# Bank-by-bank first and last chunks, a smaller first load of V and rearranged final stores in a grouped-query attention kernel

## The chip, the cores and the metric

The kernel runs on one core of a Trainium2 chip. The metric is device time of one execution in microseconds (us). Before the change three runs gave a median of 522.89 us (522.8 to 523.7). A run's time stands about 1.75 us above the span of its trace (524.22 against 522.5, 523.1 against 521.4), so the two can be turned into each other. The rounds of the experiments ran on four chips (numbers 8, 3, 15 and 5 in the record), so a time is compared with that of the kernel before in the same rounds; medians over all rounds mix chips.

## The reference

```python
B, Hq, Hkv, Sq, Sk, D = 16, 32, 8, 288, 512, 128      # bf16
k = jnp.repeat(k, Hq // Hkv, axis=1)
v = jnp.repeat(v, Hq // Hkv, axis=1)
scores = jnp.einsum("bhqd,bhkd->bhqk", q, k) * D ** -0.5
p = softmax(scores, axis=-1)
return jnp.einsum("bhqk,bhkd->bhqd", p, v)
```

## The kernel before

There are 128 groups (a batch and a head of K and V). The four heads of Q of a group are 9 tiles of 128 rows. The scores are computed transposed, keys on the partitions, in 3 chunks of 1536 columns (three PSUM banks) a group, 384 chunks in all. TensorE computes chunk n's scores, ScalarE exponentiates them into SBUF, and TensorE multiplies a batch of 3 tiles by V three chunks later. V carries a column of ones, so the sum of a row comes with the product; VectorE takes its reciprocal and evicts. For 62 of the chunks VectorE also computes 120 columns of the exponential. Parts that the argument touches, with cuts marked:

```python
# the first transfers of the sync engine (q0: Q of group 0 in two parts)
first = [lambda i=i: op_q0(i) for i in range(2)]
first += [lambda: op_q(1), lambda: op_k(0, 2), lambda: op_q(2), lambda: op_v(0, None, 2, UG), lambda: op_q(3)]
# and of ScalarE's queue
op_kd(eng, 0); ...; op_kd(eng, 1)            # K of groups 0 and 1, transposed by TensorE
op_v(0, eng, 0, 2)                           # V of groups 0 and 1

# TensorE
for n in range(NS):
    if n == 2: op_warm(4, P, ps_o[:, 0])
    op_s(n)                                  # scores: wait for K, Q and the exponential of chunk n-2
    ...
    if n == 2: op_kt(1, range(NJ), 1)        # transposes of K of group 1; VectorE copies them
    if n >= LAG: op_pv(n - LAG)              # batch n-3 times V
...
# sync engine, at the very end
eng.wait_ge(sem["s_flag"], 1)
eng.load(reg, flag_i[:])
for (s, n) in need(eng, stored()):           # 12 waits: every buffer of the output, and the last stores
    eng.wait_ge(s, n)
eng.br_ne(reg, 0, ...)                       # a rare other path if a sum was out of range
```

## Time and profile before

| | before, first profile |
|---|---|
| time of the profiled execution, span | 524.22, 522.5 us |
| median of three timed runs | 522.89 us |
| TensorE, ScalarE busy | 510.6, 513.4 us |
| Q of group 1 lands | 9.74 us |
| first P times V matmul | 10.52 us |
| last eviction ends | 520.00 us |
| from there to the end of the span | 2.48 us |

The kernel has three parts: a start until TensorE and ScalarE are both full, a steady state, and a tail after the last eviction. The first P times V matmul and the end of the last eviction mark the borders. The lines of the page and of the views stand in the prediction.

### The profile page before, as it was taken

To read this page: it belongs to the slowest core of one execution; us is meant where nothing else is said; L and a number is where in the kernel's file an instruction comes from. 1 tells how busy PE (TensorE), PEld (TensorE's weight loads), DVE (VectorE), ACT (ScalarE), POOL (GpSimd) and SP (SyncE) were. 2 spreads that over 40 slices of the span, in tenths; PEclk is the share of its full clock that TensorE was granted. 3 is DMA by queue.
4 is the path that set the end of the run, shared out by engine and by line. 5 is a ranking of instruction groups with operands and counts; after the bars stand their busy time and mean duration, and the time that the engine had idled before them with its cause. 6 is when DMAs were issued, how large, how long until landed. Compare 5 with 4: busy or idle time off the path is not lost.

```text
span 522.5 us, 15279 instructions
## 1 busy us (share of the span) xinstructions
PE 510.6 (98%) x6124; PEld 395.5 (76%) x6230; DVE 363.0 (69%) x1309; ACT 513.4 (98%) x389; POOL 79.8 (15%) x135
## 2 busy tenths in 40 slices
PE   7999999999999999999999999999999999999997
PEld 4777777777777777777777777777777777777776
DVE  1767677677677677676776776767767767767765
ACT  6999999999999999999999999999999999999996
POOL 2111111111111111111111111111111111111110
PEclk9999999999999999999999999999999999999999
DMA  8999999899899999998999999999999999997212
GB/s 174 246 219 242 260 188 226 208 225 260 208 202 273 224 184 266 241 204 219 205 267 214 199 226 230 232 230 203 238 195 235 224 218 210 205 211 179 77 69 92
DMA packets 253109, 110.05 MB, mean 211 GB/s; under 512 B 219760, under 2 KB 236784, under 8 KB 253040
## 3 DMA queue, kind: packets, MB, share of 16 engines
q1 hardware_dynamic: 252480, 108.56, 96.7%
q8 instruction: 49, 0.80, 0.7%
q10 hardware_dynamic: 560, 0.52, 0.5%
q14 instruction: 20, 0.16, 0.1%
HBM read 17.04 MB, written 37.75 MB: 105 GB/s over the span
## 4 chain that ended last, share of the span: by engine, by line
PE 96%; DMA 1%; issue 1%; SPq 0%; DVE 0%
PE ps_o L446 50%; PE ps_s L409 45%; DMA qt_sb<-in_q_dram 1%; PE ps_o L420 1%; SPq L316 0%; DVE o_sb L550 0%; DVE rl_sb L540 0%; DVE o_sb L560 0%; PE ps_o L636 0%; DVE bad_sb L586 0%; DVE flag_i L705 0%; DVE bad_sb L583 0%
## 5 line engine op out<-in xcount | busy, mean ns | idle before, releaser
L481 ACT ACTIVATE pt_sb<-ps_s 128x1536 bf16<-128x1536 f32 (+2 forms) x385 | 510.9, 1444 | 1.4 <-PE ps_s L409 1.4
L446 PE MATMUL ps_o<-v_sb,pt_sb 128*128 128x129 bf16 x4596 | 322.9, 220 | 1.3 <-DVE o_sb L550 0.2
L446 PEld LDWEIGHTS ps_o<-v_sb,pt_sb 128*128 128x128 bf16 x4596 | 283.7, 98 | 49.9 <-DVE o_sb L550 0.4
L409 PE MATMUL ps_s<-qt_sb,kt_sb 128*128 128x512 bf16 (+2 forms) x1430 | 290.6, 320 | 6.4 <-DMA qt_sb<-in_q_dram 1.9
L550 DVE TENSOR_TENSOR o_sb<-ps_o,rl_sb 128x384 bf16<-128x384 f32 x383 | 212.6, 555 | 8.9
L409 PEld LDWEIGHTS ps_s<-qt_sb,kt_sb 128*128 128x128 bf16 x1536 | 124.0, 98 | 63.5 <-ACT pt_sb L481 2.2
L540 DVE RECIPROCAL rl_sb<-ps_o 128x3 f32<-128x3 f32 x383 | 68.5, 179 | 137.0 <-PE ps_o L446 137.0
L533 POOL COPY v_sb<-vd_sb 128x512 bf16<-128x512 bf16 x128 | 78.8, 616 | 430.5 <-PE ps_o L446 416.2
L514 DVE SCALAR_TENSOR_TENSOR u_sb<-u_sb,m_sb 128x120 f32<-128x120 f32 x124 | 34.5, 278 | 0.0
L521 DVE SCALAR_TENSOR_TENSOR pt_sb<-u_sb,e_sb 128x120 bf16<-128x120 f32 x62 | 17.5, 283 | 2.1
L514 DVE SCALAR_TENSOR_TENSOR u_sb<-m_sb 128x120 f32<-128x120 f32 x62 | 17.2, 277 | 0.0
L492 DVE TENSOR_SCALAR y_sb<-ps_o 128x120 f32<-128x120 f32 x62 | 15.7, 253 | 0.0
L505 DVE TENSOR_SCALAR m_sb<-t_sb 128x120 int32<-128x120 int32 x62 | 13.8, 223 | 2.1
L505 DVE TENSOR_SCALAR e_sb<-t_sb 128x120 int32<-128x120 int32 x62 | 13.4, 217 | 0.0
L420 PE MATMUL ps_o<-qt_sb,kt_sb 128*128 128x120 bf16 x62 | 13.4, 216 | 0.0
L498 DVE TENSOR_SCALAR t_sb<-y_sb 128x120 int32<-128x120 f32 x62 | 13.2, 213 | 0.0
L420 PEld LDWEIGHTS ps_o<-qt_sb,kt_sb 128*128 128x128 bf16 x62 | 6.1, 98 | 7.3
L385 DVE COPY kt_sb<-ps_o 128x128 bf16<-128x128 bf16 (+2 forms) x3 | 1.0, 336 | 6.2 <-PE ps_o L378 6.1
L391 PE MATMUL ps_o<-z_sb 128*128 128x512 bf16 (+1 forms) x9 | 2.7, 447 | 1.3 <-DVE z_sb L667 1.3
L578 DVE TENSOR_REDUCE st_sb<-rl_sb 128x1 f32<-128x72 f32 (+1 forms) x16 | 3.5, 216 | 0.0
L576 DVE TENSOR_REDUCE st_sb<-rl_sb 128x1 f32<-128x72 f32 (+1 forms) x16 | 3.4, 215 | 0.0
L475 ACT ACTIVATE pt_sb<-ps_s 128x512 bf16<-128x512 f32 x1 | 0.6, 597 | 2.3 <-PE ps_s L409 2.3
(31 smaller groups left out, 11.0 us busy)
## 6 DMA issues: line engine op xcount, KB each, us to landing
out_dram<-o_sb SPq DMA_DIRECT2D x127, 288.0 KB, 3.5
vd_sb<-in_v_dram SPq DMA_DIRECT2D x31, 512.0 KB, 5.3
qt_sb<-in_q_dram SPq DMA_TRANSPOSE x129, 4.7
kt_sb<-in_k_dram SPq DMA_TRANSPOSE x32, 5.4
out_dram<-o_sb SPq DMA_DIRECT2D x3, 96.0 KB, 1.6
kd_sb<-in_k_dram ACTq DMA_DIRECT2D x2, 128.0 KB, 2.7
vd_sb<-in_v_dram ACTq DMA_DIRECT2D x1, 256.0 KB, 6.0
vd_sb<-in_v_dram SPq DMA_DIRECT2D x1, 256.0 KB, 3.1
```

Of the source, the lines that this page charges most:

```text
L409: ins = emit(eng, w_x, lambda: eng.matmul(ps_s[:, n % 2, c:c + w], kt_sb[:, sl, j, gi, :], qg[:, t * P:t * P + w], start=True, stop=True))
L420: emit(eng, [("s_ev", n - LAG - 1)], lambda: eng.matmul(ps_o[:, (n - LAG) % 2, BANK - W:BANK], kt_sb[:, (g // UG) % NSLOT, j, g % UG, :], ...
L446: ins = emit(eng, w_x, lambda: eng.matmul(outs(r)[:, a, :], pt(g, t, j), v_sb[:, sl, gi * NJ + j, 0:DV], start=(j == 0 and a == 0), stop=( ...
L481: emit(eng, waits, lambda: eng.activation(d, s, ACTF.Exp, scale=scale)).then_inc(sem["s_e"], 1)
L492: emit(eng, [("s_yb", nth(n) - NB), ("s_pv", n - LAG + 1)], lambda: eng.tensor_scalar(out=y_sb[:, b], in0=ps_o[:, (n - LAG) % 2, BANK - W: ...
L498: emit(eng, [("s_ym", 2 * (nth(n) - NB)), ("s_y", nth(n))], lambda: eng.tensor_scalar(out=t_sb[:, b], in0=y_sb[:, b], scalar1=Y_MUL, scala ...
L505: emit(eng, [("s_yp", nth(n) - NB), ("s_yb", nth(n))], lambda: eng.tensor_scalar(out=dst[:, b], in0=t_sb[:, b], scalar1=mask, scalar2=bits ...
L514: lambda: eng.scalar_tensor_tensor(out=u_sb[:, b, x], in0=src, scalar=QUARTIC[x], in1=m, op0=ALU.add, op1=ALU.mult)
L521: lambda: eng.scalar_tensor_tensor(out=pt_sb[:, n % NPT, CH - W:CH], in0=u_sb[:, b, 2], scalar=QUARTIC[3], in1=e_sb[:, b].bitcast(FP32), o ...
L533: emit(eng, waits, lambda: eng.tensor_copy(v_sb[:, sl, gi * NJ:(gi + 1) * NJ, 0:D], vd_sb[:, sl, gi].rearrange("p (j d) -> p j d", d=D))). ...
L540: emit(eng, [("s_pv", r + 1)], lambda: eng.reciprocal(rl_sb[:, TPC * r:TPC * (r + 1)].unsqueeze(2), outs(r)[:, :, D:DV])).then_inc(sem["s_ ...
L550: emit(eng, waits, lambda: eng.tensor_tensor(out=o_sb[:, g % NO, t0:t0 + TPC, :], in0=outs(r)[:, :, 0:D], in1=rl_sb[:, TPC * r:TPC * (r + ...
```

## The change

Its intent is to shorten the start (smaller exponentials that begin sooner, less V in front of Q) and the tail (smaller last stores, waits for stores taken before the flag is ready). The core of the diff:

```diff
-  op_q(1), op_k(0, 2), op_q(2), op_v(0, None, 2, UG), op_q(3)
+  op_q(1), op_k(0, 2), op_v(0, None, 1, UG), op_q(2), op_q(3)
-  op_v(0, eng, 0, 2)
+  op_v(0, eng, 0, 1)
...
-  if n == 0:  (512, then 1024 columns)
-  if n == NS - 1:  parts = [(0, CH - BANK), (CH - BANK, CH)]
+  if n < 2 or n == NS - 1:
+      parts = [(x, x + BANK) for x in range(0, CH, BANK)]
...
+  FINE = NG - 3
-  for g in range(LASTG): ... op_store(g)
-  for i in range(NC): ... op_store(LASTG, i)
+  for g in range(FINE): ... op_store(g)
+  for r in range(NC * FINE, NS):
+      sp.append((r + LAG + 2.6, lambda r=r: op_store(r // NC, r % NC)))
+  sp.append((NS - 1 + LAG + 2.5, op_stored))          # 9 waits, before the last store
-  for (s, n) in need(eng, stored()):                  # after the flag
+  for (s, n) in need(eng, [("s_ol", 16 * NC * (NG - FINE))]):
...
-  z_sb [P, BANK]
+  z_sb [P, P], broadcast; op_warm(2, P, ps_o[:, 1]) added
```

(The exponential's old lines are abridged to what they do.) The waits of the last batches of P times V were also made to follow the single banks.

## The prediction

> **What bounds the kernel now.** I read the page first. TensorE (510.6 us busy) and ScalarE (513.4 us) are both at 98% of a span of 522.5 us, so nearly all of the time is one steady state and the change, which touches its two ends only, can win no more than what the ends waste. The table of stages says how much that is:
>
> ```profile
> core 0: us, PE busy (x) PEld busy (x) DVE busy (x) ACT busy (x) POOL busy (x), PEclk, DMA share, GB/s
> 8.00:12.00 4.00, 2.07 (x20) 1.44 (x22) 0.99 (x3) 2.85 (x3) 1.17 (x2) 1.00 1.20 238
> 26.00:122.00 96.00, 94.95 (x1147) 73.84 (x1165) 68.39 (x248) 96.00 (x73) 14.79 (x24) 1.00 1.07 226
> 518.00:522.50 4.50, 1.53 (x26) 1.23 (x23) 2.11 (x8) 0.37 (x1) 0.00 (x0) 0.90 0.38 131
> ```
>
> From 26 to 122 us (one of four equal stretches) ScalarE never rests and TensorE is busy 94.95 of 96 us. A chunk costs 12 matmuls of P times V, 0.68 us, and 0.65 us of scores, 1.33 us in all; six chunks of ScalarE's (five of 1536 columns, one of 1416) take as long. Neither is touched there. Between 8 and 12 us TensorE has 2.07 us of work in 4. The chain of waits over the first 12 us tells why:
>
> ```profile
> 2.21 1.26 SPq L316
> 3.46 0.05 issue
> 3.51 6.23 DMA qt_sb<-in_q_dram
> 9.74 0.14 issue
> 9.88 0.81 PE ps_s L409 x3
> 10.69 0.68 PE ps_o L446 x12
> ```
>
> The transposing load of Q of group 1 is issued at 3.51 us and lands at 9.74, after 6.23 us, where the median of all 129 such loads is 4.7. The scores of chunk 3 (the first chunk of group 1) start 0.14 us later, and from there on the chain is TensorE without a gap. ScalarE in the timeline of the same stretch:
>
> ```profile
> 5.01 0.60 ACT L475 ACTIVATE pt_sb<-ps_s 128x512 bf16<-128x512 f32 x1 [2.27 <-PE ps_s L409]
> 5.86 3.71 ACT L481 ACTIVATE pt_sb<-ps_s 128x1024 bf16<-128x1024 f32 x3 [0.26 <-PE ps_s L409]
> 10.72 5.38 ACT L481 ACTIVATE pt_sb<-ps_s 128x1536 bf16<-128x1536 f32 x4 [1.15 <-PE ps_s L409]
> ```
>
> It finishes chunks 0, 1 and 2 at 9.57 us and stands still for 1.15 us until chunk 3's scores exist. So the start of the steady state is set by a DMA, and not by the exponentials of the first two chunks, in front of which ScalarE lost 0.26 us. The end, in the chain of waits from 514 us:
>
> ```profile
> 516.24 0.69 PE ps_o L446 x12
> ...
> 517.17 0.57 DVE o_sb L550
> 517.74 0.05 issue
> 517.79 0.87 PE ps_o L446 x12
> ...
> 518.90 0.56 DVE o_sb L550
> ...
> 519.58 0.42 DVE o_sb L560
> ```
>
> The last but one batch of P times V starts at 517.79 because the eviction before the previous one ends at 517.74 and frees its PSUM bank, not because of an exponential: in the timeline ScalarE's last big one (1024 columns) begins at 516.30 and lasts 1.13 us, so it is over at 517.43. The final 512 columns are over at 517.92, and the matmuls that need them come last, around 519. After the last eviction (about 520.0) the last store goes out at 520.10. DVE's flag is ready at 520.78, the sequencers read it until 521.28, and only then does the sync engine pass its waits for stores:
>
> ```profile
> L225 SPq EVENT_SEMAPHORE  x6: 17/28/28, 521.3 to 522.0; - x6
> out_dram<-o_sb SPq DMA_DIRECT2D x3, 96.0 KB, 1.6
> ```
>
> The first line is the list of instructions of the line with the store waits: six semaphore instructions from 521.3 to 522.0 us. The second is from the DMA issues: a store of 96 KB lands 1.6 us after issue, so the last one at 520.10 + 1.6 = 521.70.
>
> **What the Trainium skill says.** "ScalarE: Activation LUTs", section "What ACT_TABLE_LOAD costs", gives an ACTIVATE with immediate scale and bias 186 ns + 0.833 ns per column, back-to-back ones overlapping by about 93 ns. That is 612, 1039 and 1466 ns for 512, 1024 and 1536 columns; the trace shows 597, 1024 and 1444 to 1459 ns, and the next one starting 0.92 us after the one of 1024 columns. It agrees, so I take 0.50, 0.92 and 1.34 us from start to start. "DMA: Bandwidth & Descriptors", section "Issuing engines are not separate DMA queues", says that transfers begun by different engines run on the same 16 DMA engines and interleave. The trace fits: V of groups 0 and 1 is issued on ScalarE's queue at 3.58 us, 0.07 us after Q of group 1, and takes 6.0 us, about as long as the Q load beside it. The same page, section "Anatomy of one DMA", puts most of a small transfer's time, about 2 us, on the confirmation of the write; here 1.6 us for 96 KB, so smaller or earlier-split stores cannot land much faster. "TensorE: Matmul & The Clock Gate", section "What's actually happening", says that TensorE runs at half clock until a free-running window of about 3.4 us was busy. The trace agrees: the weight loads before the 512-column warm-up matmuls start 0.43 us apart, while three score matmuls at 9.88 us take 0.81 us in all, pipeline included.
>
> **The change part by part.**
>
> 1. *Only V of group 0 at first.* 128 KB fewer on ScalarE's queue beside Q of group 1; V of groups 1 to 3 (384 KB) follows on the sync queue behind K of groups 2 and 3, so behind Q of group 1. From 4 to 8 us the stage table (read for this) gives 184 GB/s. 128 KB is 131 KB of 1000 bytes, and 131 / 184 = 0.71 us of the shared engines. Part of it was not in front of Q's last packets, since Q's data need not wait for V's last; I count 0.6 us. Q then lands at about 9.1 instead of 9.74, the scores of chunk 3 start near 9.25, and the whole steady state moves up by 0.6 us. This is on the path. The other side: Q of group 2 now stands behind 384 KB of V. Before, it was issued at 6.29 and landed 5.1 us later, at about 11.4. About 256 KB more in front at 238 GB/s (the stage above) is 1.1 us, and 0.5 us is gained back: about 12.0. It is needed at 13.87 - 0.6 = 13.3 us, when chunk 6 starts. V of group 1 is needed at the same time and should land near 11. Both hold, with a little over 1 us to spare.
>
> 2. *Chunks 0 and 1 bank by bank.* Chunk 0: before, starts at 5.01 and 5.86, next chunk at 6.78. After, 5.01, 5.51, 6.01, so chunk 1 could start at 6.5. Chunk 1 then costs 3 x 0.50 = 1.50 instead of 1.34, so chunk 2 starts at 8.0 instead of 8.11: 0.1 us won, in front of a wait of 1.15 us. On the path: 0.0, unless Q lands before about 8.4.
>
> 3. *Warm-up.* The zero tile shrinks from 512 to 128 columns, so its memset (0.27 us) should cost about 0.1 and warm-up start 0.15 us sooner; two small matmuls (0.11 us each at half clock) fill the gap before K's transposes at 3.24 us. Whatever this does to the clock changes the scores of chunks 0 and 1, which lie before the wait for Q. On the path: 0.0.
>
> 4. *Last chunk bank by bank.* Three pieces of 512 instead of 1024 + 512: 3 x 0.50 against 0.92 + 0.50, so it ends 0.08 us later, at 518.0, still ahead of the matmuls that need it; and the first pieces were not waited for. 0.0.
>
> 5. *Last three groups stored batch by batch.* Six batches of 96 KB more instead of two stores of 288 KB; the last store stays the last, with the same size and trigger. 0.0 to 0.05.
>
> 6. *Store waits early.* Of twelve waits after the flag, one stays. It can pass when the last store has landed and its count is seen, 521.70 + 0.14 (the delay seen with Q above) = 521.84, where the last semaphore instruction now starts at 522.0 and the branch after it ends about 0.1 later: 0.2 to 0.25 us won. But the nine waits now stand between the store of the last but one batch (issued 519.48, busy to 519.82) and the last. At some 0.07 us a pair they run to about 520.15, so the last store may go out 0.1 us late. Net 0.1 to 0.2, I take 0.15.
>
> Sum: 0.6 + 0.15 = 0.75 us of 522.89, so 522.1.
>
> **Rivals.** (a) *The bank-by-bank exponentials pay.* If the slow stretch of DMA was mostly V's doing, Q lands before 8.4, and chunk 3 is bound by ScalarE. The whole idle time of 1.15 us goes, and the 0.1 of part 2: with the tail 1.4 us, 521.5. For it: 6.23 us against a median of 4.7; at the median Q would land at 8.2. Against it: the DMA share stays above 1.2 after V has landed at 9.6, so the engines are full anyway. (b) *Q does not move.* If Q was held up by its own transposes and by K of groups 2 and 3 on the same queue, both of which stay, only the tail is won: 522.7. For it: those are untouched and the larger part of the bytes. (c) *The wait moves on to Q of group 2 or V of group 1*, now behind 384 KB. TensorE then waits at chunk 6 and gives back what it won: 522.5 to 523.5. Against it is the slack of 1.3 us worked out above. (d) *The early waits delay the last store by more than they save*: 0 to +0.2 us, on top of any of these.
>
> **Range and chances.** Middle 522.1; (a) gives the lower end, 521.2 with some luck in the tail; (b), with the 0.9 us by which the runs before differ among themselves (522.8 to 523.7), gives the upper, 522.9. A change of 2% would be 10.5 us; the idle time in front of the steady state and behind it is not that large even if all of it went. Within 2%: 0.98; each other side 0.01.
>
> **What would show each step.** Part 1: Q of group 1 landing near 9.1 and ScalarE's idle time before chunk 3 near 0.5 us. Part 2: three activations of 512 columns in chunks 0 and 1, about 0.5 us apart, chunk 2 starting near 8.0. Part 4: the last batches of P times V still waiting for the eviction. Part 6: one semaphore wait after the flag, the last store going out 0.1 us later relative to the last eviction, the end about 0.15 us sooner relative to it. The steady stretch must keep 1.33 us a chunk. I am wrong if a gap of TensorE opens near chunk 6, if Q lands at 9.7 again or before 8.4, or if any stretch between 26 and 506 us changes.

## The result, and the profile after

The changed kernel took 523.5 us (median of 4 runs, 523.3 to 525.26) against 522.92 (4 runs). The ratio was 1.0015, with a 95% interval of 0.9992 to 1.0039: the same within 2%, as I had said, but outside my range of 521.2 to 522.9. Here and below a ratio is the mean time of one kernel's fast runs over that of the other's of the same rounds, so it is not quite the ratio of the medians quoted. Over all rounds the kernel before has 59 runs with a median of 523.12 us, and the changed kernel 10 with 523.48.

Yet the first profile of the changed kernel had the shorter span, 521.8 against 522.5. The chain of waits of its first 12 us (start, duration, what):

```profile
2.21 4.29 DMA qt_sb<-in_q_dram
6.49 0.05 issue
6.54 0.82 PE ps_s L421 x3
7.36 0.22 PE ps_o L402 x4
7.58 0.66 PE ps_s L421 x6
8.24 0.24 PE ps_o L389 x4
8.48 0.02 issue
8.50 0.43 DVE kt_sb L396
8.94 0.09 issue
9.03 0.81 PE ps_s L421 x3
```

Q of group 1 is no longer in this chain; in this trace it landed at 8.48. Instead the chain begins with the second half of Q of group 0, issued at 2.21 and landed at 6.49 us. From it hang the scores of chunk 1, the warm-up matmuls, the scores of chunk 2, the transposes of K of group 1, VectorE's copy of those and only then the scores of chunk 3. ScalarE in the timeline of the same stretch:

```profile
5.02 1.08 ACT L491 ACTIVATE pt_sb<-ps_s 128x512 bf16<-128x512 f32 x2 [2.29 <-PE ps_s L421]
5.99 0.60 ACT L497 ACTIVATE pt_sb<-ps_s 128x512 bf16<-128x512 f32 x1
6.96 1.09 ACT L491 ACTIVATE pt_sb<-ps_s 128x512 bf16<-128x512 f32 x2 [0.37 <-PE ps_s L421]
7.93 8.71 ACT L497 ACTIVATE pt_sb<-ps_s 128x512 bf16<-128x512 f32 x7
```

The idle time of 1.15 us before chunk 3 is gone; 0.37 us stand before chunk 1. In the tail, the last three stores of the kernel before read:

```profile
L342 SPq DMA_DIRECT2D out_dram<-o_sb x3: 332/332/332, 518.4 to 520.1; - x3
```

The last of them goes out 0.10 us after the last eviction, which ends at 520.00. In the changed kernel the waits of the sync engine from 516 us on, and the lines of its semaphore instructions and stores, read:

```profile
SPq L227 <- DMA out_dram<-o_sb: 0.8, 1, 0.8
...
L351 SPq EVENT_SEMAPHORE  x3: 27/28/28, 519.0 to 519.2; - x3
...
L343 SPq DMA_DIRECT2D out_dram<-o_sb x9: 332/332/333, 510.3 to 519.7; - x9
```

The last eviction ended at 519.14. The early waits ran from 519.0 on, and the last of nine small stores went out at 519.69, 0.55 us after that eviction instead of 0.10. After the flag the branch then waited 0.8 us for that store. The tail was 2.63 us, not shorter than 2.48 but longer.

### The profile page after: what moved, and what is told of

Its sections match the earlier page's. It is cut to its first block, busy times and chain, and to the rows that moved or that the text cites. A ratio compares the mean times of both kernels' runs of the same rounds, so it can differ in the third digit from the quotient of the medians.

```text
span 521.8 us, 15393 instructions
## 1 busy us (share of the span) xinstructions
PE 516.2 (99%) x6232; PEld 395.6 (76%) x6232; DVE 362.6 (69%) x1309; ACT 513.6 (98%) x393; POOL 79.4 (15%) x135
## 4 chain that ended last, share of the span: by engine, by line
PE 98%; DMA 1%; DVE 1%; SPq 0%; issue 0%
PE ps_o L460 50%; PE ps_s L421 47%; DMA qt_sb<-in_q_dram 1%; PE ps_o L432 1%; SPq L317 0%; DVE o_sb L566 0%; DVE rl_sb L556 0%; DVE kt_sb L396 0%; DVE o_sb L576 0%; PE ps_o L389 0%; PE ps_o L654 0%; PE ps_o L402 0%; DVE bad_sb L602 0%; DVE flag_i L723 0%; DVE bad_sb L599 0%
## 5 line engine op out<-in xcount | busy, mean ns | idle before, releaser
L421 PE MATMUL ps_s<-qt_sb,kt_sb 128*128 128x512 bf16 (+2 forms) x1536 | 309.9, 324 | 1.3 <-DMA qt_sb<-in_q_dram 0.7
L491 ACT ACTIVATE pt_sb<-ps_s 128x512 bf16<-128x512 f32 x6 | 3.4, 634 | 2.7 <-PE ps_s L421 2.7
L402 PE MATMUL ps_o<-z_sb 128*128 128x128 bf16 (+1 forms) x11 | 2.9, 422 | 1.1 <-DVE z_sb L685 1.1
```

The costliest lines, as they stand in the source:

```text
L421: ins = emit(eng, w_x, lambda: eng.matmul(ps_s[:, n % 2, c:c + w], kt_sb[:, sl, j, gi, :], qg[:, t * P:t * P + w], start=True, stop=True))
```

## The experiments

For each run I read from its trace when the two halves of Q of group 0, K of group 1 and Q of group 1 landed, the first P times V matmul, and the tail, by which I mean the time from the end of the last eviction to the end of the span. A load has landed when the last of the sixteen completion counts that the trace logs for it has come. One number is the same everywhere: from the first P times V matmul to the end of the last eviction it was 509.47 or 509.48 us in 16 traces and 509.49 in one. So the steady state and the handling of the last chunk change nothing, and time is start plus tail plus a constant.

What ends the start can be read too. In all 17 traces the scores of chunk 3 begin either 0.14 us after Q of group 1 has landed (7 traces) or 0.10 us after VectorE has finished its copy of the transposed K of group 1 (the other 10), whichever is later. Both kinds stand in the chains above and below. That copy follows the scores of chunk 2 on TensorE, these follow the scores of chunk 1, and these need the second half of Q of group 0.

| run | time, median | kernel before, same rounds | Q0, second half | K1 | Q1 | first P times V | tail |
|---|---|---|---|---|---|---|---|
| before (first profile) | 522.89 | | 5.27 | 6.17 | 9.74 | 10.52 | 2.48 |
| changed (first profile) | 523.5 | 522.92 | 6.49 | 5.59 | 8.48 | 9.67 | 2.63 |
| null_before | 523.1 | 523.23 | 5.80 | 5.57 | 8.61 | 9.39 | 2.48 |
| after_again | 523.34 | 523.23 | 5.66 | 5.45 | 8.49 | 9.27 | 2.80 |
| v_only | 523.28 | 523.23 | 6.42 | 5.57 | 8.13 | 9.60 | 2.48 |
| tail_only | 523.49 | 523.23 | 5.94 | 5.76 | 8.87 | 9.65 | 2.61 |
| after_waits_earlier | 522.8 | 523.04 | 6.55 | 5.50 | 8.06 | 9.73 | 2.07 |
| after_old_v | 523.19 | 523.04 | 5.76 | 5.54 | 8.55 | 9.34 | 2.61 |
| after_old_first_exp | 523.48 | 523.04 | 6.37 | 5.50 | 8.26 | 9.54 | 2.69 |
| fine_only | 523.11 | 523.04 | 6.07 | 5.85 | 8.72 | 9.80 | 2.37 |
| tail_waits_earlier | 522.7 | 523.13 | 5.15 | 6.62 | 9.86 | 10.64 | 2.07 |
| v0_after_q1 | 522.76 | 523.13 | 6.33 | 6.06 | 7.30 | 9.69 | 2.07 |
| after_old_last_exp | 523.39 | 523.13 | 6.37 | 5.47 | 7.72 | 9.54 | 2.83 |
| kd1_late | 523.08 | 523.17 | 5.13 | 8.07 | 7.10 | 9.72 | 2.07 |
| after_look | 523.62 (1 run) | 523.17 | 6.46 | 5.65 | 8.38 | 9.64 | 2.78 |
| null_look | 523.05 (1 run) | 523.17 | 5.65 | 5.47 | 8.57 | 9.35 | 2.48 |
| kd1_before_q1 | 523.51 | 523.11 | 5.48 | 6.61 | 7.88 | 9.45 | 2.06 |

My theory after the result was that the first profile of the kernel before had caught a slow start (theory A); the rival was a cost outside the trace (theory B).

**null_before**: the kernel before, unedited.

> The kernel before, run against itself: it measures the noise of a comparison, and whether a run of a kernel with the profiler and one without give the same time. Both theories expect a ratio of 1.000 if the two columns of times are of the same kind. Theory A (the two medians of the result are not comparable, because the span of the profiled execution fell from 522.5 to 521.8 us while the timed median rose from 522.92 to 523.5): the runs of this label stand 0.5 to 1.5 us above those of the kernel before, ratio 1.001 to 1.003, though it is the same kernel. Theory B (they are comparable, the change costs 0.6 us outside what the trace shows): ratio 0.999 to 1.001.

Ratio 0.9997 (0.9984 to 1.0010). Its runs stood where those of the kernel before stood, so the medians are comparable, and theory A is wrong in that form. It is right in another: the span of this profile was 521.4 us, 1.1 less than that of the first profile of the same code. The chain of waits of its start:

```profile
3.51 5.11 DMA qt_sb<-in_q_dram
8.61 0.14 issue
8.75 0.81 PE ps_s L409 x3
9.56 0.68 PE ps_o L446 x12
```

The load of Q of group 1 took 5.11 us here and 6.23 in the profile that I predicted from. ScalarE did not stop at all before chunk 3:

```profile
5.01 0.60 ACT L475 ACTIVATE pt_sb<-ps_s 128x512 bf16<-128x512 f32 x1 [2.28 <-PE ps_s L409]
5.67 10.69 ACT L481 ACTIVATE pt_sb<-ps_s 128x1024 bf16<-128x1024 f32 x8
```

Eight activations in 10.69 us without a gap: the idle time of 1.15 us, which I wanted to see shrink, does not exist in an ordinary execution.

**after_again**: the changed kernel, unedited.

> The changed kernel unchanged, in more rounds. Theory A: its spans are 0.5 to 1.0 us below those of the null run of the same chip, ratio to the null run 0.998 to 0.999. Theory B: its times are 0.4 to 0.8 us above the null run's, ratio 1.001 to 1.0015.

Ratio 1.0001 (0.9988 to 1.0014), median 0.24 us above the null run's. Theory A's figure is missed, B's size is not reached. Start 9.27 (0.12 sooner than the null run), tail 2.80 (0.32 later).

**v_only**: the V lines of the diff alone, on the kernel before.

> Kernel before with only the change of the V loads (group 0 alone at first, groups 1 to 3 ahead of Q of group 2). By my prediction the whole win in front of the steady state is this: Q of group 1 lands 0.6 to 1.2 us sooner than 9.74, ScalarE's idle time before chunk 3 falls from 1.15 us to 0 to 0.5, time 0.6 to 1.0 us below the null run. Rival (the bank by bank exponentials are needed for the win): 0.0 to 0.4 us below the null run.

Neither held: Q of group 1 landed at 8.13, 0.48 us sooner than in the null run, and the first P times V matmul came at 9.60, 0.21 later. The second half of Q of group 0 had landed at 6.42, and ScalarE waited 0.85 us before chunk 1. The completion counts in the packed trace (no view prints them) say more: fifteen of the sixteen of that half had come by 5.78, and one alone was late. The V of groups 1 to 3, which this edit moves as well, was issued only at 6.77, so it cannot have made that count late. Ratio 1.0014 (0.9999 to 1.0029); two of six runs took 525.1, 1.8 us more than the others. No such run was profiled, so what they are stays open.

**tail_only**: the store and wait lines of the diff alone, on the kernel before.

> Kernel before with only the stores of the last three groups batch by batch and the early store waits. Prediction: 0.1 to 0.2 us below the null run. Rival (d), which the trace of the changed kernel favours, since its last store went out 0.41 us before that of the kernel before while the last eviction ended 0.86 us before: the last store is issued 0.4 to 0.5 us later after the last eviction than before, and the time is 0.0 to 0.3 us above the null run.

The rival held in the trace: last store 0.54 us after the last eviction, tail 2.61. The time, 0.39 us above the null run's median, is a little more than the 0.0 to 0.3 that it named.

**after_waits_earlier**: the nine waits two stores further forward.

```diff
-        sp.append((NS - 1 + LAG + 2.5, op_stored))
+        sp.append((NS - 3 + LAG + 2.5, op_stored))
```

> The changed kernel with the nine early store waits moved two stores forward, between the stores of the third and the second last batch but one, where the sync engine is idle for about 1 us. Theory (the tail of the changed kernel is longer because the waits, 0.7 us of them with a stall of 0.37 us in their middle, stand between the last two stores): the last store goes out 0.1 us after the last eviction again instead of 0.54, the span ends 2.15 to 2.25 us after that eviction (before 2.48, changed 2.6 to 2.8), 0.35 to 0.5 us below the changed kernel. Rival (the stall belongs to the sequencer's place in the program or to the transfers and not to these waits): still 2.5 us or more.

The last store went out 0.04 us after the last eviction and the tail fell to 2.07. The same lines as above, of this run:

```profile
SPq L227 <- DMA out_dram<-o_sb: 0.4, 1, 0.4
...
L351 SPq EVENT_SEMAPHORE  x4: 17/28/28, 517.4 to 517.6; - x4
...
L343 SPq DMA_DIRECT2D out_dram<-o_sb x9: 332/332/332, 510.3 to 519.2; - x9
```

The waits are now over at 517.6, long before the last store. The time was 522.8 against 523.04 (ratio 0.9996, 0.9983 to 1.0009, so not clear of noise), though this start was one of the slower ones. The rival was right on one point: the stall moved. In every trace a gap of 0.346 to 0.349 us stands before the 336th instruction that the trace has of the sync engine, whatever that instruction is. In the kernel before it is a wait after the flag, in the changed kernel a wait before the last store, here a store with time to spare.

**after_old_v**: the changed kernel with the V lines undone.

> The changed kernel with the V loads as in the kernel before (groups 0 and 1 at first). Theory (the V loads do little, the long landing of 6.23 us in the first profile was that one execution's): first P times V matmul at 9.3 to 9.7 us, time within 0.3 us of the changed kernel. Rival (my prediction: halving V moves Q of group 1 by 0.6 us): Q lands 0.4 us or more later than the 8.49 us of the changed kernel, first P times V near 10, time 0.4 to 0.8 us longer.

The theory held: 9.34 us, time 0.15 below after_again's median, in other rounds and on another chip. The rival would have needed Q at 8.9; it landed at 8.55.

**after_old_first_exp**: the changed kernel, chunk 0 as 512 + 1024 columns and chunk 1 as 1536.

> The changed kernel with the exponentials of chunks 0 and 1 as before (512 + 1024 columns, then 1536). Theory (hidden in front of the wait for Q): ScalarE reaches chunk 2 0.1 to 0.4 us later, but chunk 3 starts when its scores do, first P times V within 0.3 us of 9.3 to 9.7, time within 0.2 us of the changed kernel. Rival: 0.3 us or more longer.

Held: chunk 2's exponential started at 8.62, against 8.41 and 7.65 in the first two profiles of the changed kernel. The first P times V matmul came at 9.54, between those two's 9.67 and 9.27. Its ratio to the kernel before, 1.0015 (1.0003 to 1.0027), is the only one here whose interval leaves out 1; one of its six runs took 525.21 us.

**fine_only**: stores batch by batch, all waits after the flag.

```diff
-                for (s, n) in need(eng, stored()):
+                for (s, n) in need(eng, stored() + [("s_ol", 16 * NC * (NG - FINE))]):
```

> Kernel before with the last three groups stored batch by batch, but all store waits left after the flag. Theory: nothing gained or lost, the span ends 2.45 to 2.5 us after the last eviction, as in the kernel before (2.48), last store 0.1 us after it. Rival (the smaller stores cost in the tail by themselves): 2.6 us or more.

Tail 2.37, 0.11 less than the 2.48 of the kernel before: with two buffers fewer to wait for, and the stall right after the flag is read, the branch is reached 1.97 us after the last eviction instead of 2.07. The small stores themselves cost nothing.

**tail_waits_earlier**: the kernel before with the small stores and the waits as in after_waits_earlier.

> Kernel before with the stores of the last three groups batch by batch and the nine store waits moved forward, between the stores of the third and the second last batch but one; start as in the kernel before. Theory (the tail is fixed by the sync engine's own sequence: waits plus one stall of 0.35 us that sits before the same instruction of its program in all traces so far): the span ends 2.05 to 2.2 us after the last eviction, 0.3 to 0.4 less than the 2.48 of the kernel before; time 522.5 to 522.8, 0.3 to 0.4 us below it, whatever the start does. Rival (the tail gain of the run with the changed start was luck of that start): no gain, 523.0 or more.

Held: tail 2.07, median 522.7 against 523.13, ratio 0.9992 (0.9978 to 1.0005). Its profiled execution, at 523.94 the slowest of its five, had a slow start like the first profile of the kernel before:

```profile
3.51 6.35 DMA qt_sb<-in_q_dram
```

So a slow start is no property of one profile: two of the seven profiles with the old V loads have it, and none of the other ten. In both, K of group 1 was issued later (3.22 and 3.12 us) than in the thirteen other traces that issue it from ScalarE's queue (2.98 to 3.09), because K of group 0, for which that issue waits, had landed later. Of the 59 runs of the kernel before, 6 took over 523.65 us.

**v0_after_q1**: as after_waits_earlier, V of group 0 issued by the sync engine behind Q of group 1.

```diff
-  op_q(1), op_k(0, 2), ...
+  op_q(1), op_v(0, None, 0, 1), op_k(0, 2), ...
-            op_v(0, eng, 0, 1)
```

> The changed kernel with the waits moved forward as in the run above, and V of group 0 taken off ScalarE's queue and issued by the sync engine right behind Q of group 1. Theory (V of group 0 alone, on the other queue at 3.4 us, runs beside the second half of Q of group 0 and makes its last packets late, 6.3 us in the mean of five profiles against 5.8 with the old V loads; so Q of group 1 lands 0.6 us sooner in the mean but nothing is won): the second half of Q of group 0 lands before 5.7 us, Q of group 1 before 8.3, first P times V at 8.9 to 9.3 us, time 522.0 to 522.5. Rival (it is not V that makes it late, or V of group 0 now comes too late itself): 9.3 us or later, 522.7 or more.

Q of group 1 landed at 7.30, 1.3 us before the null run's, and the start was no better (9.69), because the second half of Q of group 0 still landed at 6.33. The rival held (9.3 us or later, 522.7 or more), and my theory that V of group 0 on the other queue delays it fell.

**after_old_last_exp**: the changed kernel, last chunk as 1024 + 512 columns.

> The changed kernel with the last chunk's exponentials as before (1024 + 512 columns). Theory (not on the path, since the last batches wait for an eviction): the time from the last exponential's start to the last eviction moves by less than 0.05 us, the last batch but one of P times V still starts 0.05 us after an eviction ends; time within 0.2 us of the changed kernel's 523.3 to 523.5. Rival (bank by bank pays or costs there): 0.15 us or more either way between the last but two batch and the last eviction.

Held: 509.48 us between the borders of the steady state, as in all others, the last but one batch again 0.05 us behind an eviction, time 523.39. The bank-by-bank last chunk does nothing.

**kd1_late**: as v0_after_q1, and K of group 1 issued by the sync engine behind Q of group 1.

> The run with V of group 0 behind Q of group 1, and K of group 1 issued by the sync engine behind Q of group 1 too, so that ScalarE's queue carries only K of group 0. Theory (the completion of the second half of Q of group 0 is held up by what the other queue moves meanwhile, K of group 1 and V): it lands before 5.5 us. Rival (its own queue sets it, Q of group 1 right behind it): 5.7 to 6.6 us as in the seven profiles with the changed V loads. Under both, K of group 1 lands later than 6.1 us and its transposes may set chunk 3 (first P times V 9.3 to 10 us), so the time is not the point, 522.5 to 523.3.

The theory held: 5.13 us. With that the table shows a pattern. In the four traces where K of group 1 landed at 6.17 or later, the second half of Q of group 0 landed at 5.48 or sooner; in the other thirteen K of group 1 landed at 5.45 to 6.06 and that half at 5.65 or later. In each trace only one of the two is early. That they compete for something is my reading; the traces do not show for what. The win was eaten at once by the next wait, in the chain of its start:

```profile
4.92 3.15 DMA kd_sb<-in_k_dram
8.07 0.05 issue
8.12 0.40 PE ps_o L389 x4
8.51 0.56 issue
9.08 0.81 PE ps_s L421 x3
```

Now K of group 1, at 8.07, holds chunk 3.

**after_look** and **null_look**: one more profile of each kernel.

> Another profile of the changed kernel. If the lateness is real: second half of Q of group 0 lands at 6.2 us or later, Q of group 1 at 8.5 or sooner, first P times V 9.3 to 9.7. If it is chance: anything from 5.2 to 6.1. Both: the span ends 2.6 to 2.8 us after the last eviction.

> Another profile of the kernel before. If the difference is real: second half of Q of group 0 at 5.2 to 6.1 us, Q of group 1 at 8.5 to 8.9 (or 9.7 and more in a slow start as in the first profile, with K of group 1 after 6.1 us), first P times V 9.3 to 9.8 (or 10.5). Both: the span ends 2.48 us after the last eviction.

Both fell as the lateness being real foresaw: 6.46 and 8.38 us with the changed loads, 5.65 and 8.57 with the old ones. After_again (5.66) stays the exception: the other six profiles with V of group 0 alone on ScalarE's queue have that half at 6.37 to 6.55.

**kd1_before_q1**: K of group 1 between the second half of Q of group 0 and Q of group 1.

> As the run before, with K of group 1 issued between the second half of Q of group 0 and Q of group 1, all on the sync queue. Theory (nothing of another queue holds up the second half of Q of group 0; K of group 1 is early enough for its transposes; then the end of chunk 1's exponentials, near 8.1 us, and V of group 0 are what is left): second half of Q of group 0 before 5.5 us, K of group 1 before 6.5, Q of group 1 before 7.9, first P times V at 8.8 to 9.2 us, with the short tail 522.2 to 522.6 us, 0.5 to 0.9 below the kernel before. Rival (the order inside one queue makes no difference to when the second half of Q of group 0 completes, the run before was a lucky one; or V of group 0 is late): first P times V at 9.3 us or later, 522.7 to 523.1.

The rival's last clause held. The scores of chunk 3 started at 8.27, the soonest of all traces, and then the chain is:

```profile
5.60 3.12 DMA vd_sb<-in_v_dram
8.73 0.05 issue
8.78 0.62 POOL v_sb L549
9.40 0.05 issue
9.45 0.85 PE ps_o L460 x12
```

V of group 0 landed at 8.73, its copy ended at 9.40, and the first P times V matmul came at 9.45. The median of its five runs was 523.51, above even the rival's 522.7 to 523.1, although the profiled one took 522.73. With the same tail the other four must have had worse starts, but they are not traced.

## Why the prediction was wrong

Two steps failed. The 0.6 us of part 1 was to come out of a gap that most executions do not have, and the next wait stood right behind it. And part 6 put waits between the last two stores at too low a cost. I predicted 0.6 + 0.15 us won; in the traces the start came 0.16 us later (within its spread) and the tail took 0.26 us longer.

**The base it subtracted from.** The step that failed first is in part 1 and the chain of waits before it: "Q of group 1 ... lands at 9.74", and an idle time of 1.15 us that could be cut. Both were right for that trace and wrong for the kernel. The profiled execution took 524.22 us and the median run 522.89, and most of the excess lay in just this gap: in the two other profiles of the unedited kernel (523.1 and 523.05 us) the first P times V matmul came at 9.39 and 9.35 us, not 10.52. What I predicted to win by the V loads was a thing that most runs did not have. How much there was to win can be estimated from the rule above: in those two profiles VectorE's copy of K of group 1 ended at 8.26 and 8.58 us, so chunk 3 could have begun at 8.36 and 8.68 at best, 0.38 and 0.02 us sooner than it did, however soon Q of group 1 came.

**Part 1, the V loads.** The mechanism was half right. Leaving out the two slow starts, the five profiles with the old V loads (two of the kernel before, tail_only, after_old_v, fine_only) have Q of group 1 at 8.55 to 8.87, mean 8.66. The seven with V of group 0 alone on ScalarE's queue have it at 7.72 to 8.49, mean 8.22. That is 0.44 us sooner; I had 0.6. In five of the seven it is before 8.4, the premise of rival (a), yet the win of (a) did not come. For the second half of Q of group 0 went from a mean of 5.84 to 6.33, 0.49 later, and VectorE's copy of K of group 1, which hangs on it, set chunk 3 in six of the seven. The first P times V matmul went from 9.51 to 9.57, a difference well inside the spread of either group (9.34 to 9.80 and 9.27 to 9.73). None of my rivals named this wait. It was invisible in the first profile, because in a slow start that half lands early (5.27) and everything behind it late. The other side of part 1, Q of group 2 "about 12.0" with slack, held: 12.11.

**Parts 2, 3 and 4** were right to come to 0.0 on the path. Part 2 is shown by after_old_first_exp and part 4 by after_old_last_exp. Part 3 was not taken alone. The traces say only that the first score matmul starts at 4.23 to 4.36 us with either warm-up.

**Part 5** was right: fine_only's small stores did not delay the last one.

**Part 6, the early waits**, had the wrong sign. I put the delay of the last store at 0.1 us and the gain after the flag at 0.2 to 0.25. Measured, the last store went out 0.54 to 0.55 us after the last eviction instead of 0.10, in every trace that has this tail. The tail became 2.61 to 2.83 us instead of 2.48. The mis-sized term is "at some 0.07 us a pair": the pairs do cost that, but the stall of 0.35 us comes on top. (The 0.14 us for seeing the last store, taken over from Q, was too long: in the changed kernel the branch starts 0.02 us after that store has landed.) In the profile before, it lay among the waits after the flag (they run from 521.3 to 522.0, 0.7 us for six instructions), and I did not ask why. That was rival (d), with a larger size than I gave it.

The sum for the changed kernel, from its three profiles against the two ordinary ones of the kernel before: start 9.53 against 9.37 us, tail 2.74 against 2.48, so 0.16 + 0.26 = 0.42 us longer. The pooled medians say 523.48 - 523.12 = 0.36. Only the 0.26 of the tail is clear of the spread; the three starts of the changed kernel alone differ by 0.40.

**A better version.** The tail with the waits two stores forward measures 2.06 or 2.07 us in five traces, 0.41 less than before. Some 0.06 of it is another detail: the diff also swaps the order of the last store's two waits, and the store goes out 0.03 or 0.04 us after the last eviction instead of 0.10, in fine_only too. The ten runs of the two kernels with only that mended (after_waits_earlier and tail_waits_earlier) have a median of 522.80 us, against 523.12 for the kernel before. Each alone has an interval that includes 1, so by time it is not clear of noise. The shorter tail is: it is there in each of the five traces.

**What stays open**: why the second half of Q of group 0 is late with less V, even with V on another queue; what makes a slow start; and what the executions near 525.2 us are (4 among the 32 runs with V of group 0 alone on ScalarE's queue; among the 79 with the old V loads one is above 525, at 526.1). The first question is narrower than it looks: in the six late profiles with V of group 0 alone on ScalarE's queue the first of the sixteen counts of that half comes at 5.42 to 5.54 us, no later than with the old loads (5.38 to 5.59 in the five ordinary profiles), and only the last one to five come late, after a pause of 0.47 to 0.74 us. What has to be explained is a few late counts, not a slow load.

## What to carry to other kernels

Before a gap in a profile is counted as winnable, compare the profiled execution's own time with the median of the others: a gap in the first microseconds, where transfers race, may belong to that one execution. In a start-up where several loads feed one chain, moving one load up shows the next one, so list all landings against the time at which each is needed, not only the one that the chain names. Waits whose counts have long been reached still take the issuing engine time (here about 0.07 us for an instruction that holds two). They must not be put between the last two stores; put them where that engine is idle anyway.

## What the Trainium skill lacked or had wrong

- "Runtime: NRT & Kernel Launch", section "Instruction fetch mechanics": it says that instructions are refilled in blocks of 256 and that crossing a block is mostly hidden. Here the sync engine shows, in all 17 traces, a gap of 0.42 to 0.43 us before its 80th traced instruction and of 0.35 us before its 336th. They are 256 apart, which fits the page, though no run isolates the cause. It was not hidden in the tail, where it stood before the last store; the page gives no figure for the gap.
- "DMA: Bandwidth & Descriptors", section "Queues, rings and completion order": it says that a completion increment lands only after every earlier write of the same DMA engine, across its queues. kd1_late agrees (5.13 us with the other queue's transfer moved away, 5.65 to 6.55 in the traces where that landed early), but does not prove this cause. Nor does v_only, though it fits: fifteen counts of that half had come by 5.78 us and one came at 6.42. No page says how far landings spread from one execution to the next: the same load of Q, issued at 3.51 us by unedited code, landed at 8.57, 8.61 and 9.74.
